# Gate weights loaded in both partition halves, GpSimd's copies placed between its loads, early work ordered by landings: funnel attention followed by a multiplicative FFN

## The chip, the core and the metric

One core of a Trainium2 chip runs the whole program. The metric is the device time of one execution in microseconds, the median of several runs. The core's engines are TensorE (PE, with its weight loads shown apart as PEld), VectorE (DVE), ScalarE (ACT), GpSimd (POOL) and SyncE (SP); each takes its own instructions in order. In this kernel GpSimd issues all loads from memory, and SyncE issues the DMA transposes and nearly all stores.

## The reference

```python
batch, n_heads, seq, head_dim = (8, 8, 1152, 64)
q_pool = q.reshape(B, H, S // 2, 2, D).mean(axis=3)
scores = (1 / sqrt(D)) * np.matmul(q_pool, k.transpose(0, 1, 3, 2))
attn = softmax(scores)                       # along the keys
x = (attn @ v), heads side by side           # 4608 tokens x 512
a = x @ w1                                   # 512 x 1024
b = x @ w2                                   # 512 x 1024
out = ((a * b) @ w3) @ w_out                 # 1024 x 1024, 1024 x 512
```

The inputs are float32, the result is 4608 x 512 float32. The kernel works in float16 with float32 sums; its loads change the type on the way.

## The kernel before

**Attention.** The 64 heads are taken as 32 pairs (a pair P is two heads of one batch, `u` is the head in the pair). A pair has 576 pooled queries and nine blocks of 128 keys, so 9 x 576 = 5184 columns of scores for each head; these columns of all pairs are cut into 324 chunks of 512. A pair is thus 10.125 chunks. For each chunk, `scores` (L274) multiplies keys and queries, one head in each half of the PE's rows, into one of two PSUM buffers `psc`; `expo` (L291) has ACT take the exponential of the 128 x 1024 buffer into the ring `er`. Chunk c+2 cannot be multiplied before the exponential of chunk c has left its buffer. Two bursts per pair, `attend(P, 1)` (36 matmuls) and `attend(P, 0)` (54, L305 and L314), multiply the exponentials with the values `vt`, some 2 and 6 chunks after the pair's last chunk; `normalize` (L329) divides on DVE and issues from SP the DMA transpose of the result `xn` into `xT` (L341), the FFN's input. Where two batches are done, the ninth block of rows goes through `rems` into `xR` (L323) in the same way.

**Preparing a pair.** `load(P)` has GpSimd load k and q of pair P and v of pair P-1 (L116, L108, L123; 288 KB each as float16). For pairs 0 to 8 keys and queries are turned by PE (`prep_stage`, `prep_pe`); `copy_k` puts the keys in order first, on DVE for pairs 1 to 6 and on GpSimd for 7 and 8. From pair 9 on `prep_dma` (L154) does it without PE, all in GpSimd's and SP's queues:

- GpSimd copies the keys into `kc` (L159); SP transposes `kc` into `kT` by DMA (L160);
- GpSimd adds neighbouring queries into `qp` (L143); SP transposes `qp` into `qT` by DMA (L162);
- GpSimd copies the values into `vt` (L152);
- for pairs up to 27, GpSimd copies one element of `kT` into `seen` (L166), which makes its queue wait until the transpose of the keys has landed, and only then issues the loads of pair P+5 and goes on to pair P+1.

**Loads and their semaphores.** GpSimd's loads use eight completion semaphores in turn, so each load waits at its issue until the one eight places before it has landed.

**FFN.** Early on `w3` is turned by PE (`w3_transpose`, L441) and multiplied with `w_out` to `T16` (tile `pT`, L470), once, so that the FFN ends in one product. For each batch `add_unit` (L474) queues 16 gates (`pg`, L506: eight products with `w1` and eight with `w2` into one bank, then a copy and a multiplication into `gT`, L490 and L498) and the row products with `T16` (`pp`, L527). The remainder rows of four batches make a second unit of width 128 behind the first one (batches 3 and 7). A gate's products run in one half of the PE's rows, and the input's heads lie in one half or the other; so `w1sb` and `w2sb` keep each weight twice, once in each partition half. `load_ffn` (L369) loads the first copy; `swap_halves` (L376) makes the second by a product with the permutation matrix `swap` (L384) and a copy on DVE or ACT (L390, L387): 16 of them.

**What sets the order.** The program is written out by hand (`manual_schedule`): a planner in the kernel (L660 to L718) keeps a clock for each PE half and for DVE, emits the next chunk of scores when its exponential is due, and between chunks takes products from the queues `prep` and `ffn` (`step`, L555). What it emits is fixed at build time: each engine runs its instructions in that order, whatever the real landings are. `STAGE`, `PREP`, `early`, `events` and `WEIGHTS` (L637 to L646) say at which point of the pair count or of the planner's clock loads are issued and staged work begins; `ended` (L327) opens a batch's gates 8.0 or 6.5 us (planner's clock) after its last division.

Of the kernel before, what the change touches and what calls it, by code (L numbers as in the profile page):

```python
# [8 lines left out]
FP16 = mybir.dt.float16  # L9
# [14 lines left out]
def kernel(  # L24
# [11 lines left out]
    nc = tc.nc  # L36
# [30 lines left out]
    swap = const.tile([128, 128], FP16)  # L67
# [28 lines left out]
    def take():  # L96
        return spare.pop(0)[1]
# [71 lines left out]
    kcs, kc_done = {}, {}  # L169
# [4 lines left out]

    def prep_stage(P):

        def copy_k(eng=nc.vector):
            eng.tensor_copy(out=new_kc(P).rearrange("p j u d -> p u j d"), in_=kst.pop(P))
        jobs.append((560, lambda: pool_q(P)))
        if P < 7:  # L180
            jobs.append((280, copy_k))
        else:
            copy_k(nc.gpsimd)
            kc_done[P] = max(clock) + 3.0
# [36 lines left out]
    def prep_rest(tb):  # L221
        nc.vector.tensor_copy(out=kcs[0][:, 3:NJ].rearrange("p j u d -> p u j d"),
                              in_=kst[0][:, :, 3:NJ])
        keys(0, tb, range(3, NJ))
        nc.vector.tensor_copy(out=kT[0][:, 3:NJ].rearrange("p j f -> p (j f)"),
                              in_=tb[:, 0:768])
        copy_v(0)
        del kst[0], kcs[0]
# [134 lines left out]
    def load_w(dst, src):  # L363
        nc.gpsimd.dma_start(out=dst, in_=src.rearrange("(c p) f -> p c f", p=128))

    def load_ffn(h):
        cols = slice(512 * h, 512 * h + 512)
        for dst, src in ((w1sb, moe_w1), (w2sb, moe_w2)):
            nc.gpsimd.dma_start(out=dst[:, 0, :, cols],  # L369
                                in_=src.rearrange("(c p) f -> p c f", p=128)[:, :, cols])  # L370
            swaps[h].extend((dst, c, cols) for c in range(NC))

    swaps = ([], [])
    copied = [[1e9], [1e9]]

    def swap_halves():  # L376

        half = 0 if swaps[0] else 1  # L380
        dst, c, cols = swaps[half].pop(0)
# [3 lines left out]
        clock[:] = [max(clock) + 0.22] * 2  # L385
        if c % 3 == 1:
            nc.scalar.copy(out=dst[:, 1, c, cols], in_=t)  # L387
            done = exp_done[-1] = max(exp_done[-1], clock[0] + T_SEM) + 0.6
        else:
            nc.vector.tensor_copy(out=dst[:, 1, c, cols], in_=t)  # L390
            done = vector(512, clock[0])
        give(n, done)
        if not swaps[half]:
            copied[half][0] = done + T_SEM

    def swap_due():
        half = 0 if swaps[0] else 1
        free = 3 if prep[0] or prep[1] else 2
        return bool(swaps[half]) and max(clock) > WEIGHTS[half] and len(spare) >= free and (
            spare[0][0] < min(clock))  # L400

    w3T = {}

# [37 lines left out]
    def w3_transpose(c):  # L441

        w3T[c] = ffp.tile([128, NF, 128], FP16, tag="w3T", bufs=4, name="w3T")
        ready = [1e9]
        left = [2]
        landed = 13.0

        def out(t, at, h):
            nc.vector.tensor_copy(out=w3T[c][:, :, 64 * h:64 * h + 64],
                                  in_=t[:, 0:512].rearrange("p (a f) -> p a f", f=64))  # L450
            done = vector(256, at)
            left[0] -= 1
            if left[0] == 0:
                ready[0] = max(done + T_SEM, landed)
# [9 lines left out]
        def copy(t, at):  # L464
            nc.vector.tensor_copy(out=T16[:, c, :], in_=t)
            del w3T[c]
            return vector(512, at)

        def product(t, s, n, start, stop):
            nc.tensor.matmul(t, w3T[c][s, n, :], wosb[s, n, :], start=start, stop=stop,  # L470
                             skip_group_check=True)
        add(ffn, Block("pT", NF, (0, 1), copy), 0.216, [ready], product)

    def add_unit(n, x, places, ready, final=False):  # L474
# [7 lines left out]
        def gate(ft, h):  # L482
            def mul(t, at):
# [8 lines left out]
                if h not in gT:  # L492
                    gT[h] = ffp.tile([128, NF, 256], FP16, tag="g", bufs=4, name="gT")
# [10 lines left out]
            def emit(t, s, i, start, stop):  # L504
# [5 lines left out]
                [ready, copied[2 * ft // NF]], emit)  # L510
# [24 lines left out]
        for h in range(2):  # L535
            for ft in range(NF):
                gate(ft, h)
# [3 lines left out]
    def add_batch(b, ready):  # L541

        k, o, end = (b // 2) % 2, 256 * (b % 2), b == B - 1
        add_unit(256, lambda s, m: xT[s, m, k, o:o + 256],
                 [(h, 128 * i, [(b, 4 * i + 2 * h), (b, 4 * i + 2 * h + 1)])
                  for h in range(2) for i in range(2)], ready)
        if b % 4 == 3:
            add_unit(128, lambda s, m: xR[s, m // 2, b // 2 - 1:b // 2 + 1, m % 2],
                     [(h, 0, [(b - 3 + h, 8), (b - 1 + h, 8)]) for h in range(2)],
                     ready, final=end)  # L550
# [63 lines left out]
    load_v(0)  # L614
# [3 lines left out]
    load_w(wosb, moe_w_out)  # L618
# [4 lines left out]
    nc.gpsimd.tensor_copy(out=swap[:, 0:64], in_=ident[:, 64:128])  # L623
    nc.gpsimd.tensor_copy(out=swap[:, 64:128], in_=ident[:, 0:64])
# [3 lines left out]
    def last_chunk(P):  # L628
        return -(-(P + 1) * PAIR // CH) - 1

    def copy_v_later(P):
# [8 lines left out]
    events = sorted(  # L640
        [(0.0, 4, load), (0.0, 3, load_w3), (0.4, 5, load), (0.4, 0, load_ffn), (1.2, 6, load),
         (1.2, 1, load_ffn), (2.3, 7, load), (4.0, 8, load), (4.75, 9, load), (5.0, 10, load),
         (5.95, 11, load), (6.95, 12, load), (7.05, 13, load)]
        + list(zip((1.75, 2.6, 3.7, 4.35, 5.1, 5.4, 6.1, 7.0), range(1, NPE),
                   [copy_v_later] * NPE)), key=lambda e: e[0])
    WEIGHTS = (47.0, 57.0)  # L646
    jobs = []
    kq_done[0] = 0.0
    bursts = sorted([(last_chunk(P) + (2 if u == 1 else 6), P, u)
                     for P in range(NP) for u in range(2)])  # L650

    def due(c):


        if bursts and (c + 1) * CH > bursts[0][1] * PAIR + RING:
            return 1e9
        P = ((c + 1) * CH - 1) // PAIR
        return max(exp_done[c - 2] if c > 1 else 0.0, kq_done.get(P, 0.0))
# [3 lines left out]
    while c < NCHUNK or bursts or ffn[0] or ffn[1]:  # L662
        h = 0 if clock[0] <= clock[1] else 1
        if bursts and (c > bursts[0][0] or c == NCHUNK) and spare and spare[0][0] < clock[h] and (
                fresh or c > bursts[0][0] + 1 or c == NCHUNK):
            attend(*bursts.pop(0)[1:])
            fresh = False
            while swap_due():
                swap_halves()
            continue  # L670
        if c >= NCHUNK or due(c) > clock[h]:
# [5 lines left out]
            if not step(h):  # L677
                if swap_due():
                    clock[:] = [max(clock) + 0.1] * 2
                    swap_halves()  # L680
                    clock[:] = [clock[0] + 0.1] * 2
                else:
                    clock[h] += 0.02
# [10 lines left out]
        exp_done.append(max(exp_done[-1] if c else 0.0, max(clock) + T_SEM) + T_EXP)  # L694
        if c == 0:
            prep_rest(rest)
        if jobs:
            n, job = jobs.pop(0)
            job()
            vector(n, 0.0)  # L700
        if staged < NPE and at >= STAGE.get(
                staged, staged - (0.95 if staged < 4 else 1.3)):
            prep_stage(staged)
            staged += 1
        while events and at >= events[0][0]:
            _, n, act = events.pop(0)
            act(n)
        todo = prepped < NP and at >= PREP.get(prepped, prepped - (
            0.65 if prepped < 4 else 0.9 if prepped < NPE else 1.9))
        if todo and prepped >= NPE:  # L710
            prep_dma(prepped)
            prepped += 1
        elif todo and prepped < staged and prepped in kcs:
            prep_pe(prepped)
            prepped += 1
        elif early and c >= early[0][0] and len(w3T) < 4:
            w3_transpose(early.pop(0)[1])
# [38 lines left out]
```

## Time and profile before

| what | value |
|---|---|
| median of 3 runs | 425.18 us (424.91 to 425.28) |
| the profiled execution | 422.81 us, of which the span is 420.7 us |
| PE busy | 402.0 us, 7666 matmuls |
| ACT busy | 330.7 us, 382 instructions; the 324 exponentials are 308.2 us of it |
| DVE, POOL busy | 219.9 us, 191.6 us |
| loads by GpSimd's queue | 33.56 MB, 51.8% of 16 DMA engines' time |
| transposes and stores by SP's queue | 24.22 MB, 36.5% |
| read from memory | 67.11 MB |

Busy times are sums over the span. The PE shows as busy nearly everywhere since its matmuls overlap; how dense it is can be read from the distance of their starts (gate products start 0.11 us apart, one in each half). The last exponential begins at 367.35 us; what follows, up to 416.9 us, is products of the last batches.

### The profile page before, as it was taken

The page shows a single profiled execution, that of the slowest core. Times are in us where ns is not written, and L with a number is a line of the kernel's source. Part 1 is how long each engine was busy: PE and PEld are TensorE (multiplying, and loading weights), DVE is VectorE, ACT ScalarE, POOL GpSimd, SP SyncE. Part 2 cuts the span into 40 slices and gives each one's busy share as a digit, 9 for nine tenths or more (in the row PEclk, how much of TensorE's full clock was granted, in tenths as well). Part 3 has the DMA queues.
Part 4 walks back from the last instruction along what each step waited for, and adds up shares of the span by engine and source line. Part 5 has one row for each costly group of instructions (what it writes and reads, how often), then busy time and mean ns, then how long its engine had stood idle before and what let it go on. Part 6 is the DMA issues. An engine that isn't in the chain of part 4 may idle for free.

```text
span 420.7 us, 17427 instructions
## 1 busy us (share of the span) xinstructions
PE 402.0 (96%) x7666; PEld 320.2 (76%) x7666; DVE 219.9 (52%) x596; ACT 330.7 (79%) x382; POOL 191.6 (46%) x209
## 2 busy tenths in 40 slices
PE   3799999999999999999999997999999999999996
PEld 1366665678778877888788886888878887888894
DVE  3266656876436654664356455466446644542432
ACT  3968888988888888888788896889888888834342
POOL 8243345762564675665645764556688100000000
PEclk9999999999999999999999999999999999999999
DMA  8999999999999999989999999999997422102021
GB/s 120 204 207 201 186 205 200 180 170 142 141 169 185 161 148 164 184 136 121 156 198 130 150 167 186 145 145 173 119 147 160 52 45 92 44 19 101 2 104 51
DMA packets 94219, 59.02 MB, mean 140 GB/s; under 512 B 64832, under 2 KB 84544, under 8 KB 94144
## 3 DMA queue, kind: packets, MB, share of 16 engines
q0 software_dynamic: 26528, 33.56, 51.8%
q1 hardware_dynamic: 67456, 24.22, 36.5%
q8 instruction: 60, 0.98, 1.0%
q10 hardware_dynamic: 160, 0.13, 0.1%
q14 instruction: 15, 0.12, 0.1%
HBM read 67.11 MB, written 9.44 MB: 182 GB/s over the span
## 4 chain that ended last, share of the span: by engine, by line
PE 92%; ACT 3%; DMA 2%; issue 1%; DVE 0%; POOL 0%; ACTq 0%; POOLq 0%
PE pg L506 30%; PE psc L287 19%; PE po L305 18%; PE pp L527 14%; PE pT L470 4%; PE po L314 3%; ACT er L293 3%; PE t L255 1%; DMA xT<-xn 1%; PE sw L384 1%; DMA kst<-in_k_dram 1%; PE w3t L458 0%; PE pp L593 0%; POOL qst L108 0%; PE tb L188 0%
## 5 line engine op out<-in xcount | busy, mean ns | idle before, releaser
L293 ACT ACTIVATE er<-psc 128x1024 f16<-128x1024 f32 x324 | 308.2, 1029 | 49.8 <-PE psc L287 43.7
L287 PE MATMUL psc<-qT,kT 64*128 64x384 f16 (+7 forms) x1152 | 132.3, 291 | 3.9 <-ACT er L293 3.5
L506 PE MATMUL pg<-xT,w2sb 64*128 64x256 f16 x1024 | 129.3, 269 | 0.0
L506 PE MATMUL pg<-xT,w1sb 64*128 64x256 f16 x1024 | 128.4, 269 | 1.0 <-DMA xT<-xn 0.9
L506 PEld LDWEIGHTS <-w1sb 64*128 64x128 f16 x1280 | 102.0, 94 | 9.9 <-issue 1.6
L506 PEld LDWEIGHTS <-w2sb 64*128 64x128 f16 x1280 | 102.0, 94 | 6.0
L527 PE MATMUL pp<-T,gT 64*128 64x512 f16 (+1 forms) x552 | 98.2, 376 | 0.0
L305 PEld LDWEIGHTS <-er 128*128 128x128 f16 x2304 | 74.6, 98 | 18.4 <-issue 15.3
L305 PE MATMUL po<-vt,er 128*128 128x65 f16 x2304 | 82.5, 194 | 2.8 <-issue 2.5
L287 PEld LDWEIGHTS <-kT 64*128 64x128 f16 x1152 | 60.9, 95 | 30.5 <-issue 15.9
L498 DVE TENSOR_TENSOR gT<-pg,asb 128x256 f16<-128x256 f32 (+1 forms) x160 | 66.2, 416 | 24.1 <-ACT asb L487 19.9
L490 DVE COPY asb<-pg 128x256 f32<-128x256 f32 (+1 forms) x119 | 48.1, 404 | 27.4 <-PE pg L506 25.7
L333 DVE RECIPROCAL rz<-po 128x4 f32<-128x4 f32 x64 | 12.1, 189 | 92.8 <-PE po L305 48.2
L143 POOL TENSOR_TENSOR qp<-qst 64x1152 f16<-64x1152 f16 x23 | 54.4, 2367 | 1.0
L527 PEld LDWEIGHTS <-gT 64*128 64x128 f16 (+1 forms) x552 | 43.0, 94 | 11.1
L166 POOL COPY seen<-kT 1x1 f16<-1x1 f16 x19 | 3.4, 181 | 83.6 <-DMA kT<-kc 83.6
L152 POOL COPY vt<-vst 128x1152 f16<-128x1152 f16 x28 | 32.1, 1149 | 6.6 <-issue 5.4
L123 POOL DMA_DIRECT2D vst<-in_v_dram x32 | 23.2, 725 | 19.1 <-DMA kst<-in_k_dram 7.2
L116 POOL DMA_DIRECT2D kst<-in_k_dram x33 | 24.0, 728 | 11.8 <-DMA kst<-in_k_dram 2.7
L487 ACT COPY asb<-pg 128x256 f32<-128x256 f32 (+1 forms) x41 | 13.1, 331 | 19.7 <-PE pg L506 18.6
L336 DVE TENSOR_TENSOR xn<-po,rz 128x256 f16<-128x256 f32 x64 | 27.2, 424 | 2.2
L159 POOL COPY kc<-kst 128x1152 f16<-128x1152 f16 x23 | 26.8, 1164 | 0.8 <-DMA kT<-kc 0.8
(62 smaller groups left out, 254.2 us busy)
## 6 DMA issues: line engine op xcount, KB each, us to landing
qst<-in_q_dram POOLq DMA_DIRECT2D x32, 288.0 KB, 6.9
vst<-in_v_dram POOLq DMA_DIRECT2D x32, 288.0 KB, 8.3
kst<-in_k_dram POOLq DMA_DIRECT2D x31, 288.0 KB, 6.0
out_dram<-osb SPq DMA_DIRECT2D x32, 256.0 KB, 3.4
w3h<-in_moe_w_dram POOLq DMA_DIRECT2D x4, 512.0 KB, 14.5
wosb<-in_moe_w_out_dram POOLq DMA_DIRECT2D x1, 1024.0 KB, 13.8
xT<-xn SPq DMA_TRANSPOSE x64, 4.7
w1sb<-in_moe_w_dram POOLq DMA_DIRECT2D x2, 512.0 KB, 15.6
```

The source lines that it names most:

```text
L116: nc.gpsimd.dma_start(out=kst[P][:, :, js[0]:js[1], :], in_=k[b, h0:h0 + 2].rearrange("u (p j) d -> p u j d", j=NJ)[:, :, js[0]:js[1], :])
L143: (eng or nc.vector).tensor_tensor(out=qps[pp][r].rearrange("p c u d -> p u c d"), in0=src[:, :, :, 0, :], in1=src[:, :, :, 1, :], op=ALU.add)
L152: (eng or nc.vector).tensor_copy(out=vts[P % 4][:, :, :, 0:D], in_=vst.pop(P))
L159: nc.gpsimd.tensor_copy(out=kc.rearrange("p j u d -> p u j d"), in_=kst.pop(P))
L287: nc.tensor.matmul(t[:, u, o:o + ln], kT[P][s, j, :], qv[s, f0:f0 + ln], start=True, stop=True)
L293: nc.scalar.activation(out=er[:, :, r:r + CH], in_=psc.pop(c), func=AF.Exp, bias=0.0, scale=SCALE)
L305: nc.tensor.matmul(po[:, VW * i:VW * i + D + 1], er[:, u, r:r + 128], vts[P % 4][:, u, j, 0:D + 1], start=(j == 0 and i == 0), stop=(j == ...
L336: nc.vector.tensor_tensor(out=xn, in0=acc[:, 0:4, 0:D], in1=rz[:, 0:4].to_broadcast([128, 4, D]), op=ALU.mult)
L490: nc.vector.tensor_copy(out=a, in_=t[:, 0:n])
L498: nc.vector.tensor_mul(out=g, in0=b, in1=a)
L506: nc.tensor.matmul(t[:, n * w:n * w + n], (w1sb, w2sb)[w][s, (m + h) % 2, m // 2, fs], x(s, m), start=start, stop=stop, skip_group_check=True)
L527: nc.tensor.matmul(t, gT[h][s, i, cs], T16[s, i, :], start=start, stop=stop, skip_group_check=True)
```

## The change

The second copy of each gate weight is loaded from memory, the two partition halves by a DMA each, in place of the 16 exchanges; the matrix `swap` goes. `w_out` is loaded in two halves of columns, and the first two products `pT` are made in two halves that wait for them. v of pair 0 is loaded after `w_out`. Loads and GpSimd's copies stand in one list `events`, at fixed places; `copy_k` of pairs 7 and 8 is one of them. Staging of pairs 1 to 8 and the transposes of `w3` are emitted by the planner's clock (`STAGE`, `W3`), looked at before each chunk (`landed`). In the batches with a remainder unit, its gates alternate with those of the first unit, and their tiles use the buffers `w3T` in place of `g`. `prep_dma` and its queueing are the same.

```diff
     def load_ffn(h):
         cols = slice(512 * h, 512 * h + 512)
         for dst, src in ((w1sb, moe_w1), (w2sb, moe_w2)):
+            heads = src.rearrange("(c s p) f -> s p c f", s=2, p=64)[:, :, :, cols]
             nc.gpsimd.dma_start(out=dst[:, 0, :, cols],
                                 in_=src.rearrange("(c p) f -> p c f", p=128)[:, :, cols])
-            swaps[h].extend((dst, c, cols) for c in range(NC))
-    def swap_halves():
-        n = take()
-        t = bank("sw", n)
-        nc.tensor.matmul(t, swap, dst[:, 0, c, cols], start=True, stop=True)
...
+            for s in range(2):
+                nc.gpsimd.dma_start(out=dst[64 * s:64 * s + 64, 1, :, cols], in_=heads[1 - s])
...
             add(ffn, Block("pg", 2 * H, (h,), mul), 0.0025 + n / 2400,
-                [ready, copied[2 * ft // NF]], emit)
+                [ready, [WEIGHTS[2 * ft // NF]]], emit)
...
+        gates = [next(u) for u in units]
         for h in range(2):
             for ft in range(NF):
-                gate(ft, h)
+                for gate in gates:
+                    gate(ft, h)
...
-    load_v(0)
     load_k(1)
     load_q(1)
     load_w3(0)
-    load_w(wosb, moe_w_out)
+    for half in range(2):
+        load_w_out(slice(256 * half, 256 * half + 256))
+    load_v(0)
     load(2)
...
+    def landed(c):
+        nonlocal staged, prepped
+        if vec < max(clock) + 0.3:
+            job()
+        if staged < NPE and max(clock) >= STAGE[staged] and kq_done.get(staged - 1, 1e9) < 1e9:
+            prep_stage(staged)
+            staged += 1
+        if prepped < staged:
+            if not jobs:
+                prep_pe(prepped)
+                prepped += 1
+        elif early and max(clock) >= W3[early[0] // 2] and len(w3T) < 4:
+            w3_transpose(early.pop(0))
...
-    early = [(14, 0), (14, 1), (19, 2), (20, 3), (26, 4), (27, 5), (33, 6), (34, 7)]
-    STAGE = {1: 0.39, 2: 1.4, 3: 2.15, 4: 2.85, 5: 3.85}
-    PREP = {1: 0.55, 2: 1.6, 3: 2.45, 4: 3.2, 5: 4.1}
-    WEIGHTS = (47.0, 57.0)
+    W3 = (5.6, 19.4, 26.4, 32.0)
+    STAGE = {1: 3.2, 2: 15.4, 3: 22.4, 4: 29.4, 5: 36.5, 6: 51.3, 7: 66.3, 8: 70.7}
+    events = [
+        (0.0, load_k, 4), (0.0, load_q, 4), (0.0, load_w3, 3), (0.4, load_v, 3), (0.4, load_k, 5),
+        (0.4, load_q, 5), (0.4, load_ffn, 0), (0.4, load_v, 4), (0.8, load_k, 6),
+        (0.8, load_q, 6), (0.8, load_ffn, 1), (1.15, copy_v_later, 0), (1.75, copy_v_later, 1), (1.8, copy_v_later, 4),
...
+        (5.3, copy_v_later, 5), (5.3, copy_k, 7), (5.3, load_v, 8), (5.4, load_k, 10),
+        (5.4, load_q, 10), (5.4, copy_v_later, 6), (5.4, copy_k, 8), (5.4, load_v, 9),
+        (5.4, load_k, 11), (5.4, load_q, 11), (5.4, copy_v_later, 7), (5.4, load_v, 10),
+        (6.4, load, 12), (6.4, copy_v_later, 8), (6.9, load, 13)]
+    WEIGHTS, WOUT = (47.5, 62.5), (9.2, 11.8)
```

In the built program PE loses the 16 products with `swap` and their weight loads, and makes 64 products `pT` of 256 columns where 32 of 512 were; DVE loses 12 copies of 512 columns and ACT four; GpSimd issues eight loads of 256 KB and one more for `w_out`, and makes two small copies less. SP has the same 168 instructions, in nearly the same order.

More of the change, by code (lines that the diff above doesn't have):

```diff
@@ L368, in load_ffn @@
         for dst, src in ((w1sb, moe_w1), (w2sb, moe_w2)):
+            heads = src.rearrange("(c s p) f -> s p c f", s=2, p=64)[:, :, :, cols]
             nc.gpsimd.dma_start(out=dst[:, 0, :, cols],
                                 in_=src.rearrange("(c p) f -> p c f", p=128)[:, :, cols])
[L371 to L400 removed]
+            for s in range(2):
+                nc.gpsimd.dma_start(out=dst[64 * s:64 * s + 64, 1, :, cols], in_=heads[1 - s])
     w3T = {}
+    second = []
     class Block:
@@ L462, in w3_transpose, with columns, copy, product @@
                 0.0285, [[0.0]], emit)
[L464 to L474, printed above, removed]
+        def columns(cols, landed):
+            m = cols.stop - cols.start
+            def copy(t, at):
+                nc.vector.tensor_copy(out=T16[:, c, cols], in_=t[:, 0:m])
+                if cols.stop == dm:
+                    del w3T[c]
+                return vector(m, at)
+            def product(t, s, n, start, stop):
+                nc.tensor.matmul(t[:, 0:m], w3T[c][s, n, :], wosb[s, n, cols], start=start,
+                                 stop=stop, skip_group_check=True)
+            add(ffn, Block("pT", NF, (0, 1), copy), 0.0025 + m / 2400, [ready, [landed]], product)
+        if c > 1:
+            columns(slice(0, dm), 0.0)
+            return
+        columns(slice(0, 256), WOUT[0])
+        second.append(lambda: columns(slice(256, 512), WOUT[1]))
+        if c == 1:
+            for part in second:
+                part()
+    def unit(n, x, places, ready, final=False):
         gT = {}
@@ L533, in rows @@
                     lambda i: [gdone[h][i]], emit)
-        for h in range(2):
-            for ft in range(NF):
-                gate(ft, h)
+        yield gate
         for h, o, to in places:
```

95 lines of the change are left out of this document (39 added, 56 removed).

## The prediction, made before the changed kernel had run

> **What bounds the kernel now.** I read the chain of waits first (the page's part 4), then ScalarE's timeline, then the chain in order of time at the two places where that timeline breaks step, then SyncE's and GpSimd's timelines there.
>
> ```profile
> PE 92%; ACT 3%; DMA 2%; issue 1%; DVE 0%; POOL 0%; ACTq 0%; POOLq 0%
> ```
>
> The PE carries the chain, but its timing is that of the exponentials. ScalarE's timeline (start, length, engine, line, operation, tiles, count, idle time before and its releaser):
>
> ```profile
> 203.25 2.85 ACT L293 ACTIVATE er<-psc 128x1024 f16<-128x1024 f32 x3 [0.51 <-PE psc L287]
> 207.18 1.02 ACT L293 ACTIVATE er<-psc 128x1024 f16<-128x1024 f32 x1 [1.08 <-PE psc L287]
> 209.12 5.76 ACT L293 ACTIVATE er<-psc 128x1024 f16<-128x1024 f32 x6 [0.91 <-PE psc L287]
> 215.38 3.77 ACT L293 ACTIVATE er<-psc 128x1024 f16<-128x1024 f32 x4 [0.51 <-PE pg L506]
> 219.98 5.76 ACT L293 ACTIVATE er<-psc 128x1024 f16<-128x1024 f32 x6 [0.82 <-PE psc L287]
> ```
>
> From 209.12 to 219.98 is an undisturbed pair: ten chunks in 10.86 us, so 11.0 us for a pair's 10.125; the short idles are the two bursts. The idle of 1.08 before 207.18 is no burst. There the chain in order of time (start, length) says
>
> ```profile
> 200.91 4.88 DMA xT<-xn
> ```
>
> The gates of batch 3 need the transposed result of pair 15. SyncE's and GpSimd's timelines show why it starts so late:
>
> ```profile
> 196.97 2.04 SPq L160 DMA_TRANSPOSE kT<-kc  x1
> 199.30 1.52 SPq L162 DMA_TRANSPOSE qT<-qp  x1
> 200.91 1.21 SPq L341 DMA_TRANSPOSE xT<-xn  x1
> ```
> ```profile
> 193.50 0.18 POOL L166 COPY seen<-kT 1x1 f16<-1x1 f16 x1 [5.03 <-DMA kT<-kc]
> ...
> 195.78 1.16 POOL L159 COPY kc<-kst 128x1152 f16<-128x1152 f16 x1
> 196.90 2.38 POOL L143 TENSOR_TENSOR qp<-qst 64x1152 f16<-64x1152 f16 x1
> ...
> 203.53 0.18 POOL L166 COPY seen<-kT 1x1 f16<-1x1 f16 x1 [3.17 <-DMA kT<-kc]
> ```
>
> In SyncE's order that transpose stands behind keys and queries of pair 18, and these wait for GpSimd. GpSimd runs a loop of its own: `seen` waits for the transposed keys, then three loads (2.1 us), the next keys' copy (1.16), their transpose. Its rounds start at 102.21 (pair 9) and, twelve later, at 237.45: 11.27 us each, no shorter than a pair's 11.0. So it runs free and cannot catch up; all it has is its lead. When it starts:
>
> ```profile
> 12.03 0.72 POOL L116 DMA_DIRECT2D kst<-in_k_dram  x1 [1.67 <-DMA kst<-in_k_dram]
> ...
> 35.38 0.77 POOL L369 DMA_DIRECT2D w1sb<-in_moe_w_dram  x1 [2.15 <-DMA w3h<-in_moe_w_dram]
> ...
> 88.39 0.72 POOL L123 DMA_DIRECT2D vst<-in_v_dram  x1 [2.81 <-DMA kst<-in_k_dram]
> 89.11 1.16 POOL L159 COPY kc<-kst 128x1152 f16<-128x1152 f16 x1
> ...
> 102.21 0.18 POOL L166 COPY seen<-kT 1x1 f16<-1x1 f16 x1 [8.28 <-DMA kT<-kc]
> ```
> ```profile
> 92.27 1.63 SPq L341 DMA_TRANSPOSE xT<-xn  x1
> 94.00 2.86 SPq L160 DMA_TRANSPOSE kT<-kc  x1
> ```
>
> Every load waits for the landing of the one eight before it: up to here the loads are one saturated queue, and pair 9's copy of keys stands behind it. Last, the chain at 258 us:
>
> ```profile
> 258.36 2.53 issue
> ```
>
> There the PE waits for nothing visible, in the middle of the 128-wide gates, its densest stretch of instructions (28 to 40 such products between two chunks, where 256-wide gates have 14 to 20).
>
> **The change, part by part.**
>
> *More loads, and the loop (the path).* The second copies are 2 x 2 loads per half of the columns, 256 KB each: 2,048 KB more, all ahead of pair 9 in the queue. The queue's rate from the rows above: between 12.03 and 35.38 the eleven loads from q of pair 1 to the third part of w3 landed, 4,576 KB in 23.35 us, 196 KB/us; between 35.38 and 88.39, 27 loads (five of 512 KB, 22 of 288), 8,896 KB in 53.0 us, 168 KB/us. So the added loads cost 10.5 to 12.2 us; I take 11.0, nearer the emptier end, since they stand at the border of the two stretches. Against that, the copy of pair 9's keys ended at 90.27 and its transpose waited until 94.00 behind the result of pair 6 (92.27). In the changed order it stands ahead of that result and of the burst before it: 3.7 us regained. The loop starts 11.0 - 3.7 = 7.3 us later. `prep_dma` is unchanged, so nine rounds later pair 18's queries, and the transpose behind them, are 7.3 late too: it lands at 205.79 + 7.3 = 213.1 where the PE waits for it. The PE reaches this wait half a chunk earlier in its work and has as little left behind it; no correction. **+7.3** (bounds: rounds vary from 9.5 to 13.0 us, so nine of them by some 3 us: +4 to +10.5). Queued behind the waiting products: the burst of pair 16 and chunk 178, thus ScalarE.
>
> *The front.* The 16 exchanges with ACT's four copies (0.59 each) and DVE's twelve (0.68) leave chunks 50 to 75. From 61.65 to 107.72 forty chunks took 46.1 us where four pairs take 43.4: 2.6 us to be had at most. The first burst ran 2.16 us against 1.27 for later ones; work now stands ahead of it, 0.9 at most. Losses: transposes of pair 1 now stand behind chunk 3, where the PE must wait for queries that landed at 13.06 and now, v of pair 0 being behind them, some 1.5 us earlier, plus 1.2 us on DVE: about 1.1 us, where the old place cost 0.5. Pair 2's key copies stand on DVE behind copies to `T16` and of v, and 32 transposes of w3 stand ahead of chunk 20 on PE: about 1.4 us. Together some -0.8 (from -3.5 to +1.5). **It counts 0**: what the PE gains before chunk 177 it spends there, waiting for the transpose. If that were on time, the cover would be gone and the front would count.
>
> *Split products `pT`.* 64 of 256 columns for 32 of 512, the same columns; 32 more weight loads (94 ns) run beside products, in a stretch that waits for exponentials. 0. GpSimd's nine more issues (0.72 each) lie in time in which its queue waits for landings. 0.
>
> *Alternating gates.* The 128-wide products no longer follow each other. The wait of 2.53 us should go: **-2.5** (bounds 0 and -2.5; the stretch becomes 1.5 times, not twice, as dense in instructions as 256-wide gates).
>
> *The end.* 372 products of 256 columns stand behind the last scores where 379 did: 7 x 0.11 / 2 = **-0.4**.
>
> Sum against the profiled execution: 422.81 + 7.3 - 2.5 - 0.4 = 427.2 us. The median of the runs shown is 2.4 above that execution, which I carry over: **429.6 us**. Later the loop doesn't bind again: pair 27's keys landed at 306.61, 5.9 us before their chunk; 7.3 late with the PE 4.8 late leaves 3.4.
>
> **The rivals.**
>
> *1. The loop absorbs it (the other side: faster).* If pair 18 is no later than before, the wait at 205 is the old one: 425.18 - 2.5 - 0.4 = 422.3. It decides while the loop's delay at pair 18 is under 2.9 us. For it: rounds as short as 9.5 us occur. Against: the mean of twelve is 11.27, and nothing else in its rows waits for the PE.
>
> *2. The visible wait of 2.5 us stays.* For it: the alternating stretch is still dense. Against: nowhere else is such a wait. 432.1.
>
> *3. Half absorbed.* Shorter rounds give back 3.6 us: 429.6 - 3.6 = 426.0.
>
> *4. Transfers into 64 partitions are slower.* q's loads go into 64 partitions and take 6.9 us from issue to landing, k's 6.0 for as many bytes: with 15% more the added loads take 12.7 us, 1.7 more: 431.3. Against: v's, into 128, take 8.3. The Trainium skill ("DMA: Bandwidth & Descriptors", Rules for kernel authors) speaks against this change: transfers to disjoint partition halves serialize, and one of 128 partitions and at least 1 MiB is best. From its table of bandwidths (138 GB/s at 64 KB, 341 at 1 MB) I estimate that 256 KB loads might run at half the rate; the added loads would then be 22 us and the sum 441. The rows of q so far don't bear that out.
>
> *That it doesn't do what it says* can be left out: the built program has the loads and lacks the exchanges.
>
> **How the numbers follow.** Forecast 0.46, rival 1 0.26, rival 2 0.10, rival 3 0.13, rival 4 0.05. The forecast's own range is 427.0 to 432.0 (the delay 4.7 to 9.7). The 8-in-10 range reaches down into rival 1 and up over rival 2: 422.0 to 432.6; below lies under half of rival 1, above some 0.06. A change under 0.2% (0.85 us) can't be told from none here. Faster: rival 1 and a little of 3, less what of 1 comes out small: 0.28. Same: 0.08. Slower: 0.64.
>
> **What would show it.** Right: the first `seen` near 109.5 us in place of 102.21; an idle of some 7 us on ScalarE before chunk 178, with `xT` as its cause; no wait of 2.5 us near the 128-wide gates; the last exponential near 372 in place of 367.35; the weights' last load landing some 11 us later. Wrong: `seen` starting before 105 (the queue is faster than its rows, or loads wait differently), rounds clearly under 11 us, or a wait at a pair's first scores (keys or queries late) that comes before the one at batch 3. If the front's losses exceed 7 us, the PE reaches chunk 177 later than the transpose, and the reason would be wrong even if the time were right.

## The result and the profile after

The changed kernel takes 431.0 us (median of 17 runs, 425.67 to 436.98) beside 425.18 us for the kernel before in the same session (17 runs, 421.93 to 427.69): a ratio of 1.0137 with a 95% interval of 1.0106 to 1.0168, some 5.8 us slower. Ratios here and below are of the fast runs alone (those within 1.5% of their kernel's fastest), medians are of all runs. The profiled execution of the changed kernel took 425.67 us, the lowest of its 17; of before it took 422.81. So that one profile shows only 2.9 us of the loss, and the experiments below begin with a second one.

The chain of waits of the changed kernel, by engine and by line, then its groups for the exponentials, the gates and `seen` (busy time, mean ns, idle time before and its cause):

```profile
span 423.5 us, 17454 instructions
...
PE 69%; DMA 24%; POOL 3%; issue 1%; DVE 1%; ACT 0%; POOLq 0%; DVEq 0%; SPq 0%; ACTq 0%
...
L290 ACT ACTIVATE er<-psc 128x1024 f16<-128x1024 f32 x324 | 307.9, 1030 | 55.6 <-PE psc L284 53.9
...
L493 PE MATMUL pg<-xT,w1sb 64*128 64x256 f16 x1024 | 124.4, 270 | 3.7 <-DMA xT<-xn 3.4
...
L165 POOL COPY seen<-kT 1x1 f16<-1x1 f16 x19 | 3.4, 179 | 80.2 <-DMA kT<-kc 80.2
```

DMA had 2% of the chain and has 24%: followed back from a wait in the middle, the chain now leaves PE and runs through GpSimd's loads to the start. That is not 24% more time; ScalarE's idle time, which was 49.8 us, is 55.6.

The start of the loop on GpSimd's timeline, and the chain in order of time there (start, length):

```profile
98.43 0.71 POOL L122 DMA_DIRECT2D vst<-in_v_dram  x1 [1.02 <-DMA kst<-in_k_dram]
99.15 1.16 POOL L158 COPY kc<-kst 128x1152 f16<-128x1152 f16 x1
...
111.01 0.18 POOL L165 COPY seen<-kT 1x1 f16<-1x1 f16 x1 [7.05 <-DMA kT<-kc]
```
```profile
99.15 1.16 POOL kc L158
100.39 2.38 POOL qp L142
102.78 10.41 DMA qT<-qp
```

`seen` of pair 9 ends its wait at 111.01 instead of 102.21. The queries of the pair land still later, at 102.78 + 10.41 = 113.19; before they took 5.7 us from an issue at 96.95. The last load of the weights lands at 74.54 instead of 64.16.

ScalarE's timeline around batch 2's gates, the chain there, and SyncE's timeline:

```profile
160.98 2.85 ACT L290 ACTIVATE er<-psc 128x1024 f16<-128x1024 f32 x3 [0.51 <-PE psc L284]
167.18 1.02 ACT L290 ACTIVATE er<-psc 128x1024 f16<-128x1024 f32 x1 [3.35 <-PE psc L284]
```
```profile
163.92 2.32 DMA xT<-xn
```
```profile
158.57 1.27 SPq L159 DMA_TRANSPOSE kT<-kc  x1
160.90 1.21 SPq L161 DMA_TRANSPOSE qT<-qp  x1
162.63 2.47 SPq L338 DMA_TRANSPOSE xT<-xn  x2
```

The input of pair 11's transpose was there at 154.93. In SyncE's order it stands behind the keys and queries of pair 14, which waited for GpSimd; it was issued at 163.92 and landed at 166.24. ScalarE stood idle for 3.35 us. The wait of 2.53 us with the cause "issue" is gone: the longest with that cause in the chain is 0.68 us, at 83.24. Around 258 us the chain reads:

```profile
256.33 0.41 PE po L311 x18
256.74 0.54 PE psc L284 x8
257.28 1.08 PE pp L514 x10
258.36 0.27 PE psc L284 x4
```

Most of what follows is read from one series (the number in front is that of the experiment): the start of an exponential in a profile less its start in the profile of before (us; positive is later). A step between two columns is time lost or won there. Batch 2's gates lie between 136 and 140, batch 3's between 176 and 184, the old 2.5 us wait between 224 and 228, pair 9's first scores between 88 and 92.

```
chunk                       44    68    92   136   140   180   184   224   228   323
   after, first profile    +1.1  +1.3  +2.4  +2.1  +5.7  +5.1  +5.0  +4.8  +2.0  +2.9
 1 after, second profile   +0.3  -0.4  +2.9  +2.8  +7.7  +7.2 +10.9 +11.3  +8.5  +8.7
 2 no second copies        +3.3   0.0  +0.9  +0.7  +5.2  +3.9  +3.8  +4.1  +1.3  +1.7
 3 no turns                 0.0  -1.5  +1.7  +3.3  +8.2  +7.0  +7.0  +6.7  +6.5  +6.5
 7 keys behind xT          +2.6  +2.0  +6.9  +7.3  +7.6  +7.3  +8.3  +8.7  +5.9  +8.0
 8 six loads later         +1.7  -1.3  +5.5  +5.8 +10.1  +9.1 +10.0 +11.7  +8.9  +9.1
 5 four output tiles       +1.4  -0.4  +2.4  +3.3  +9.3  +8.5  +8.4 +11.2  +8.4  +8.6
 4 before + turns          +0.3  +0.1  +0.1  +0.3  +0.3  -1.0  -1.1  +1.3  -1.5  +4.5
 6 before + weights twice   0.0  +8.3  +9.2  +8.8 +12.5 +11.4 +11.4 +13.4 +10.7 +14.3
10 before + keys behind xT +0.5  +0.3  +0.4  +0.2  +0.2  -1.1  -1.1  -1.1  -2.2  -2.2
 9 keys behind xT, split   +3.2  +2.1  +7.1  +6.6  +6.6  +5.7  +7.1  +8.0  +5.2  +5.5
11 before + all three      +0.8  +0.6  +0.8  +0.5  +0.5  -0.8  -0.9  +0.3  -2.5  -2.1
12 no second, keys behind  +1.4  -2.0  -1.3  -1.8  -1.8  -3.2  -2.8  +0.4  -2.4  -2.1
```

### The profile page after: what moved, and what is told of

It reads as the page before. It is cut to its first block, busy times and chain, and to the rows that moved or that the text cites. A ratio compares the mean times of both kernels' runs of the same rounds, so it can differ in the third digit from the quotient of the medians.

```text
span 423.5 us, 17454 instructions
## 1 busy us (share of the span) xinstructions
PE 399.2 (94%) x7682; PEld 316.9 (75%) x7682; DVE 210.3 (50%) x589; ACT 328.1 (77%) x377; POOL 196.9 (46%) x216
## 4 chain that ended last, share of the span: by engine, by line
PE 69%; DMA 24%; POOL 3%; issue 1%; DVE 1%; ACT 0%; POOLq 0%; DVEq 0%; SPq 0%; ACTq 0%
PE pg L493 26%; PE pp L514 14%; PE psc L284 13%; PE po L302 13%; DMA kst<-in_k_dram 10%; DMA w1sb<-in_moe_w_dram 7%; DMA vst<-in_v_dram 3%; DMA qT<-qp 2%; PE po L311 2%; DMA xT<-xn 2%; POOL qp L142 1%; POOL vst L122 0%; POOL qst L107 0%; POOL wosb L361 0%; PE pp L585 0%
## 5 line engine op out<-in xcount | busy, mean ns | idle before, releaser
L290 ACT ACTIVATE er<-psc 128x1024 f16<-128x1024 f32 x324 | 307.9, 1030 | 55.6 <-PE psc L284 53.9
L284 PE MATMUL psc<-qT,kT 64*128 64x192 f16 (+7 forms) x1152 | 130.1, 289 | 4.7 <-ACT er L290 3.2
L493 PE MATMUL pg<-xT,w1sb 64*128 64x256 f16 x1024 | 124.4, 270 | 3.7 <-DMA xT<-xn 3.4
L493 PE MATMUL pg<-xT,w2sb 64*128 64x256 f16 x1024 | 126.1, 270 | 0.0
L493 PEld LDWEIGHTS <-w1sb 64*128 64x128 f16 x1280 | 92.7, 94 | 11.5 <-issue 4.1
L493 PEld LDWEIGHTS <-w2sb 64*128 64x128 f16 x1280 | 92.0, 94 | 5.6
L514 PE MATMUL pp<-T,gT 64*128 64x512 f16 (+1 forms) x552 | 94.1, 376 | 0.0
L476 DVE COPY asb<-pg 128x256 f32<-128x256 f32 x120 | 48.4, 404 | 28.0 <-PE pg L493 26.8
L514 PEld LDWEIGHTS <-gT 64*128 64x128 f16 (+1 forms) x552 | 38.6, 94 | 17.4 <-issue 1.2
```

The source lines that it names most:

```text
L284: nc.tensor.matmul(t[:, u, o:o + ln], kT[P][s, j, :], qv[s, f0:f0 + ln], start=True, stop=True)
L290: nc.scalar.activation(out=er[:, :, r:r + CH], in_=psc.pop(c), func=AF.Exp, bias=0.0, scale=SCALE)
L476: nc.vector.tensor_copy(out=a, in_=t[:, 0:n])
L493: nc.tensor.matmul(t[:, n * w:n * w + n], (w1sb, w2sb)[w][s, (m + h) % 2, m // 2, fs], x(s, m), start=start, stop=stop, skip_group_check=True)
L514: nc.tensor.matmul(t, gT[h][s, i, cs], T16[s, i, :], start=start, stop=stop, skip_group_check=True)
```

## The experiments

All ratios are to the kernel before in the same session, with 95% intervals. A median is that of all runs of the kernel, with their range. The median of the kernel before was 425.2 to 425.8 in the sessions of experiments 1 to 11 and 423.25 in that of experiment 12, so kernels of different sessions are better compared by their ratios.

**1. The changed kernel again.**

> The changed kernel once more, unchanged. Its first profiled execution took 425.67 us and its median is 431.0, so most of what the change costs is not in that profile. Theory (GpSimd's loop starts late and then runs with little slack, 1.3 to 2.2 us ahead of the first scores of pairs 9 to 13): a slower execution shows longer waits of PE on landings of xT, kT or qT between chunks 88 and 180, 2 to 6 us more of them than the 3.4 us at batch 2's gates of the first profile. Rival (a general slowing, of every matmul or every exponential): the waits are the same and the pace between them, 10.86 us for ten chunks, is longer. Median again 429 to 433 us.

Measured: 430.92 us (429.62 to 439.73, 6 runs), 1.0119 [1.0058, 1.018]; the profiled execution took 431.43. The second row of the table says where: +3.8 at pair 9's first scores (first profile +1.2), +4.9 at batch 2's gates (+3.6), and a new +3.7 between 180 and 184. From chunk 92 on the two rows run parallel to within 0.6 us between these places, so the rival (a slower pace everywhere) falls. The new one is on the chain as

```profile
210.27 7.54 DMA out_dram<-osb
```

A store of output rows, itself issued behind transposes in SyncE's queue, lands late; VectorE waits for its tile and PE for VectorE. The theory holds for two of the three places; this third is not a landing of `xT`, `kT` or `qT`.

**2. No second copies.**

```diff
-            for s in range(2):
-                nc.gpsimd.dma_start(out=dst[64 * s:64 * s + 64, 1, :, cols], in_=heads[1 - s])
...
-  (w1sb, w2sb)[w][s, (m + h) % 2, m // 2, fs]
+  (w1sb, w2sb)[w][s, 0, m // 2, fs]
```

> The changed kernel without its eight loads of the second copies (2,048 KB fewer); every gate reads the first copy, so half of its products take the wrong half of the weights. The order of TensorE's instructions is that of the changed kernel. Theory (the loads delay GpSimd's queue): the first wait for pair 9's transposed keys is over near 101 us instead of 111, the wait for xT at batch 2's gates is gone, and the time falls by 5 to 9 us, to 422 to 426, that is to before or under it by the 2.5 us of the alternating gates. Rival (the new order of PE and of the front costs the time): 429 to 432 us, as the changed kernel.

Measured: 426.56 us (422.37 to 432.36, 12 runs), 0.998 [0.9946, 1.0013]. The time falls by 4.4 us (by the ratios, 1.0119 to 0.998, by the whole loss) and the wait at pair 9's first scores is gone (+0.1 between 88 and 92). But `seen` of pair 9 comes at 107.17, not 101, and the step at batch 2's gates stays at 4.5 us. So the loads are more than half of the loss. Whether they alone make the wait for `xT` this profile can't say: its `seen` is still 5.0 us later than in the kernel before. Experiment 12's kernel is this one up to pair 9, and there `seen` came at 101.10; the same loads ahead of it landed up to 6.5 us apart in the two executions.

**3 and 4. The turns, taken out of the changed kernel and put alone into the one before.**

```diff
-        gates = [next(u) for u in units]
-        for h in range(2):
-            for ft in range(NF):
-                for gate in gates:
-                    gate(ft, h)
+        for u in units:
+            gate = next(u)
+            for h in range(2):
+                for ft in range(NF):
+                    gate(ft, h)
```

> The changed kernel with the gates of the remainders behind those of the batch again, in place of taking turns. Theory: PE's wait with the cause issue, 2.5 us in the dense gates of 128 columns near 258 us, comes back, and the time is 2 to 3 us above the changed kernel's, 433 to 434 us. Rival 1 (the wait has gone because the instructions before it have shifted, not because of the turns): no such wait, the same 431 us. Rival 2 (the turns themselves cost, through the shared tiles): 428 to 430 us.

> The kernel before with one part of the change alone: the gates of the remainders taking turns with those of the batch. Loads and exchanges as before. Theory: the 2.5 us wait with the cause issue at 258 us goes, and the time is 1.5 to 3 us under before, 422 to 423.5 us. Rival (the wait moves to another dense stretch, or another wait takes its place at the next landing): within 1 us of before, 424.5 to 426 us.

Measured: without turns 434.37 us (429.22 to 440.84, 6 runs), 1.0144 [1.0085, 1.0202]; before with turns 429.35 us (425.71 to 432.17, 12 runs), 1.0104 [1.0063, 1.0145]. Without the turns the chain again has

```profile
264.35 2.28 issue
```

and the step of -2.8 at 224 to 228 is gone (-0.2). By the ratios the turns are worth 1.1 us here (1.0144 against 1.0119), with intervals that overlap. In the kernel before, the turns won the same 2.8 us there and lost more elsewhere: its time rose by 3.8 us where 1.5 to 3 less were expected. PE's waits and VectorE's (us in total, times, longest) name the place:

```profile
PE pg L507 <- DVE osb L521: 3.4, 1, 3.4
```
```profile
DVE osb L521 <- DMA out_dram<-osb: 8.1, 3, 4.8
```

Another 2.4 us were lost between 184 and 224, where waits with the cause "issue" of 1.28 and 0.88 us now stand at 225.76 and 238.24. The term of 2.5 us is thus right at its place, in all ten profiles with turns; what it is worth in the end depends on the stores and on such new waits, of 0.5 to 1.3 us between 210 and 260 us in five of the ten. What they are is told at the end.

**5. Four output tiles in place of three** (`tag="osb", bufs=4` in the changed kernel).

> The changed kernel with four tiles for output rows on their way to memory in place of three. In its second profile 3.7 us were lost between chunks 180 and 184 where the chain runs through a store of output rows that took 7.5 us, and VectorE waited for its tile. Theory (late stores are a good part of the run-to-run loss): the median falls by 1 to 3 us to 428 to 430, and the spread of the runs (425.7 to 439.7) gets narrower. Rival (they are rare): 430 to 432, same spread.

Measured: 430.08 us (427.2 to 433.49, 6 runs), 1.011 [1.0057, 1.0164]. Within 1 us of the changed kernel; inconclusive as to its size, and small at most.

**6. Weights loaded twice, alone in the kernel before.**

```diff
+            heads = src.rearrange("(c s p) f -> s p c f", s=2, p=64)[:, :, :, cols]
+            for s in range(2):
+                nc.gpsimd.dma_start(out=dst[64 * s:64 * s + 64, 1, :, cols], in_=heads[1 - s])
-            swaps[h].extend((dst, c, cols) for c in range(NC))
...
-            while swap_due():
-                swap_halves()
...
-    copied = [[1e9], [1e9]]
+    copied = [[47.5], [62.5]]
```

> The kernel before with one part of the change alone: the weights loaded twice and no exchanges; the front, the places of GpSimd's copies and the order of the gates as before. Theory (2,048 KB more in GpSimd's saturated queue): pair 9's keys come 7 to 11 us later than 102.2, batch 2's or batch 3's gates wait for xT, and the time is 3 to 7 us over before, 428 to 432. Rival (GpSimd's queue is delayed by the fixed places of its copies, not by the loads): pair 9's keys near 103 to 105 and 424 to 427 us.

Measured: 435.72 us (432.38 to 437.49, 6 runs), 1.0232 [1.0179, 1.0286]: more than the whole change, and more than expected. `seen` of pair 9 came at 112.82, 10.6 us late, as the theory has it. Most of the loss is another wait, though:

```profile
PE po L304 <- POOL vt L151: 8.5, 1, 8.5
```
```profile
72.93 0.72 POOL L122 DMA_DIRECT2D vst<-in_v_dram  x1 [1.84 <-DMA w2sb<-in_moe_w_dram]
73.64 1.16 POOL L151 COPY vt<-vst 128x1152 f16<-128x1152 f16 x1
```

The copy of pair 4's values stands in GpSimd's queue behind loads that wait for landings, and the burst waits for it. In the changed kernel this copy has a fixed place further forward (61.0 us), and the longest such wait is 0.6 us: the second part of the change takes this wait away.

**7. Keys and queries behind `xT` in SyncE's queue** (from pair 10 on; GpSimd's order is untouched).

```diff
-        if NPE <= prepped < NP and at >= prepped - 1.9:
+        if NPE <= prepped < NP and at >= prepped - (1.9 if prepped == NPE else 1.45):
```

> The changed kernel with the keys' and queries' transposes from pair 10 on put behind, not ahead of, the transposes xT of the pair three before in SyncE's queue (0.45 pairs later in the order). GpSimd's order is the same. Theory: xT of pair 11 is issued when its input is there (155 instead of 164 us) and batch 2's gates no longer wait: the step of 3.5 to 4.9 us between chunks 136 and 140 goes, and the time is 3 to 5 us under the changed kernel's 431. Rival 1 (keys then come too late): a wait at the first scores of pairs 12 to 14, and no gain. Rival 2 (the gates wait for something else than the order of SyncE's queue): the step stays.

Measured: 428.53 us (423.97 to 430.75, 12 runs), 1.0067 [1.0022, 1.0113]; 2.5 us under the changed kernel. The step between 136 and 140 falls to 0.3 us, on SyncE's timeline because

```profile
156.12 5.41 SPq L338 DMA_TRANSPOSE xT<-xn  x2
162.07 2.60 SPq L159 DMA_TRANSPOSE kT<-kc  x1
```

the results go first. The wait at pair 9's first scores is still there (+4.1 in this profile); pairs 12 to 14 don't wait, and of the later ones only one does, 1.02 us for its queries at 298.14.

**8. Six loads moved behind pair 9's keys and queries.**

```diff
         nc.sync.dma_start_transpose(
             out=qT[P], in_=qps[pp][o:o + 64].rearrange("p c u d -> p (c u d)"))
+        if P == 9:
+            load(12)
+            copy_v(8, nc.gpsimd)
+            load(13)
...
-        (6.4, load, 12), (6.4, copy_v_later, 8), (6.9, load, 13)]
```

> The changed kernel with the loads of pairs 12 and 13 (six, 1,728 KB) moved behind pair 9's copy of keys and sum of queries in GpSimd's queue. Theory: pair 9's transposed keys come when the loads ahead of them have landed (in five profiles their wait was over 0.2 to 0.9 us after the landing of the last load before it, at 101.8 to 111.9 us), so it is over near 101 us instead of 111, the 2 to 4 us lost at pair 9's first scores (chunks 88 to 92) come back, and the wait for xT at batch 2's gates gets shorter: 2 to 5 us under the changed kernel's 431. Rival (transposes share the DMA engines with whatever loads are under way, also those issued later): the wait still ends at 109 to 111 and the time stays within 1 us of the changed kernel's.

Measured: 437.94 us (431.83 to 447.2, 6 runs), 1.0237 [1.0168, 1.0306]: worse. The keys were issued at 90.84 instead of 100.33 but `seen` came at 106.90, after 16 us, and of the queries the chain says

```profile
93.30 21.79 DMA qT<-qp
```

They landed at 115.09; the last of the loads issued meanwhile landed at 115.20. So a transpose does not only wait for the loads issued before it: the rival is right in kind, these transposes share the engines with whatever is under way. It had neither number, though: `seen` came 2 us before the 109 to 111 it gave, and the time rose by more than its 1 us. By the Trainium skill ("DMA: Bandwidth & Descriptors", Queues, rings and completion order) each DMA engine takes packets in turn from the queues that it has work for; the 21.79 us agree with that, and a queue of its own didn't shield the transpose.

**9. Keys behind `xT`, and the loads of pair 13 behind pair 9's `seen`.**

```diff
             nc.gpsimd.tensor_copy(out=seen[:, 0:1], in_=kT[P][0:1, 0, 0:1])
+            if P == 9:
+                load(13)
             load(P + 5)
...
-        (6.4, load, 12), (6.4, copy_v_later, 8), (6.9, load, 13)]
+        (6.4, load, 12), (6.4, copy_v_later, 8)]
```

> The changed kernel with the later place of keys and queries in SyncE's queue, and with the three loads of pair 13 (864 KB) behind pair 9's seen instead of ahead of its copy of keys. Theory (pair 9's transposed keys and queries land when the loads issued before them, and those still issued after them, have landed): seen of pair 9 comes 3 to 5 us earlier, near 106 to 108 us, its first scores wait 0 to 1 us instead of 2 to 4, and the time is 1.5 to 4 us under the 428.5 with the later place alone. Rival (the loads come in the way of pair 10's or 11's transposes instead): seen of pair 9 is earlier, but the wait is at pair 10's or 11's first scores, and the time is 428 to 430.

Measured: 426.35 us (423.55 to 432.38, 12 runs), 1.0049 [0.9998, 1.0099]. The wait at pair 9's first scores is gone (+0.2 between 88 and 92; its keys were 6.4 us early). `seen` was not earlier, 111.46: this execution's front was 3 us late, and the keys' copy began at 101.10. The queries landed at 111.96, 4.9 us before those of experiment 7. But the loss has moved: 3.6 us stand between chunks 84 and 88, at a wait of 2.23 us with the cause "issue" at 109.23, and at chunk 92 both profiles are some 7 us behind. The 2.2 us between the medians are 0.8 by the ratios, with intervals that overlap: the theory is not shown.

**10 and 11. The kernel before with keys behind `xT`** (the same line), **and that with turns and four output tiles as well.**

> The kernel before with one thing changed: from pair 10 on the transposes of keys and queries stand behind, not ahead of, xT of the pair three before in SyncE's queue. Theory (xT of pair 15 stands behind pair 18's keys and queries, and batch 3's gates wait 1.1 us for it): that wait goes, 0.5 to 1.5 us under before, 424 to 425.3. Rival (keys then come later at every round, and the lead of GpSimd's loop is used up): waits at first scores, 425.6 to 428.

> The kernel before with three things: the gates in turns, the later place of keys and queries in SyncE's queue, and four tiles for output rows. With the turns alone, VectorE waited 8.1 us for stores of output rows, PE 4.4 us for VectorE, and the 2.8 us gained at chunk 228 were lost again at chunks 196 to 244. Theory (the three tiles for output rows, and stores behind transposes in SyncE's queue, are what the turns run into): these waits go, and the time is 2 to 5 us under before, 421 to 424. Rival (the turns cost in another way): 426 to 430 as with the turns alone.

Measured: 420.23 us (418.89 to 423.12, 12 runs), 0.9909 [0.9876, 0.9943], and 421.26 us (418.95 to 424.73, 12 runs), 0.9956 [0.9917, 0.9995]. Both beat both kernels. The one line of order is worth 5.0 us by the medians and 3.9 by the ratio (2.4 to 5.3), where 0.5 to 1.5 were expected. ScalarE's timeline of experiment 10 no longer has the idle of 1.08 us at batch 3's gates:

```profile
197.07 5.83 ACT L293 ACTIVATE er<-psc 128x1024 f16<-128x1024 f32 x6
203.41 3.77 ACT L293 ACTIVATE er<-psc 128x1024 f16<-128x1024 f32 x4 [0.51 <-PE psc L287]
208.01 5.76 ACT L293 ACTIVATE er<-psc 128x1024 f16<-128x1024 f32 x6 [0.82 <-PE psc L287]
```

The table has -1.3 there and -1.1 at 228 (the wait with the cause "issue" is 1.48 us instead of 2.53), and 2.2 at the end. What the ratio has beyond these 2.2 us no profile shows, and it stays open. In experiment 11 the turns' loss at the stores is gone for the most part (6.0 between 228 and 323 became 0.4), which bears the reading of experiment 4 out; three edits were made there at once, so it is not said which did it. Turns on top of the order gain nothing that these runs can tell (0.9956 against 0.9909).

**12. No second copies, and keys behind `xT`.**

> The changed kernel without the loads of the second copies (every gate reads the first copy, so half of its products take the wrong half of the weights), and with keys and queries behind xT in SyncE's queue from pair 10 on. It closes the sum: if the extra loads (through pair 9's keys and queries) and the order of SyncE's queue (through xT at batch 2's and 3's gates) are together what the change runs into, neither wait is left, the step of 4.5 us at chunks 136 to 140 that the kernel without the second copies still had is gone, and the time is 419 to 422.5 us, 4 to 7 under that kernel's 426.6 and near the 420.2 of the kernel before with the same order. Rival (the new front, or PE's new order, has a price of its own): 423.5 to 427.

Measured: 423.58 us (419.03 to 429.56, 12 runs), 0.9994 [0.9956, 1.0031]. The median is 3.0 us under that of experiment 2, but the median of the kernel before, taken beside it, was 2.3 us lower too; by the ratios (0.998 there) the order gains nothing here. In the profile both waits are gone and the sum closes: no step at pair 9 nor at batch 2, and 2.1 us under before at the end, as in experiment 10 (2.2). The time of the runs doesn't close: the median lies at the lower end of the rival's range, 3.3 us over experiment 10 (3.6 by the ratios). From 184 to 224 even this profile loses 3.2 us, among it waits with the cause "issue" of 1.0 us at 211.75 and 223.71, where experiment 10 loses nothing; whether that is what the other runs lose wasn't tried.

## Why the prediction was right, and where it was not

The direction and the time were right (429.6 forecast, 431.0 measured, in the forecast's own range), and so was the source of the loss, the added loads. The place was not: the forecast put the whole loss at batch 3's gates, an idle of 7 us before chunk 178, and there PE waited 0.25 us. That the sum came out near is in part luck. By its steps:

- **More loads, and the loop: right in kind, near in size.** The weights landed 10.4 us later against 11.0, and `seen` of pair 9 came at 111.01 against 109.5 (8.8 us late, not 7.3). Loaded twice alone, the weights made it 10.6 us late. Taken out of the changed kernel, they gave back 3.8 us of `seen` in experiment 2's profile and 9.9 in experiment 12's. One part was worth less than forecast: the 3.7 us regained in SyncE's order were there at the issue (the keys' transpose was issued 0.02 us after their copy). But the transpose took 10.63 us instead of 8.16: it landed only behind the last load ahead of it, and that one landed 9.1 us later than before.
- **"Nine rounds later pair 18's queries, and the transpose behind them, are 7.3 late too": this step failed.** The rounds from pair 9 to 18 took 10.8 us, not 11.3, and `seen` of pair 18 was 4.7 us late; so the loop gave back 4.1 us on the way, which is what rival 3 describes (3.6 there). More to the point, the loss did not wait for batch 3. The forecast said that PE reaches this kind of wait "half a chunk earlier"; with the exchanges gone, PE starts on batch 2's gates while exponential 134 runs instead of 138 (on batch 3's at 174 instead of 175). Four chunks are 4.3 us, and so batch 2's gates, which had not waited, took the wait for `xT`: 3.6 us in one profile, 4.9 in the other. In before the result had landed at 161.00 and the gates began at 163.82, 2.8 us to spare; in after it landed 5.2 us later and the gates began 2.0 us earlier. So the later loop and the earlier place both have their part, and no run parts them (in experiment 2 too the loop was 5 us late at pair 9). Experiment 7 shows that SyncE's order is what makes the transpose late.
- **A wait that the forecast named as a sign against it came.** Pair 9's first scores wait for its queries, 1.2 us in the first profile and 3.8 in the second. The forecast had followed the keys only, which in before landed 8.7 us ahead of these scores. The queries' transpose stands behind the keys' and lands, like theirs, behind the loads under way: at 113.19, 10.5 us later than before, where the scores would have started near 112.3. Experiments 2 and 12, without the added loads, have no such wait.
- **Alternating gates, -2.5: right at its place.** -2.8 in all ten profiles with turns. Without them a wait with the cause "issue" stands near this place in all four: 2.5 us before, 2.3 in experiment 3, 1.5 in 10, and in 6 two, of 1.8 and 1.9 us. That the same edit loses time at the stores in the kernel before, and that smaller waits of the kind come up elsewhere, was not foreseen.
- **The front, 0: not shown to be 0.** At chunk 44 the seven profiles with the new front and the second copies stand 0.0 to 3.2 us behind before, at chunk 68 from -1.5 to +2.1. It varies by more than the forecast's term, and its mean is a loss of 1.5 us at 44 and of 0.3 at 68. The reason for the 0 fell too: with next to no wait left at chunk 177, there was nothing to spend a gain on. (The 43.4 us that the forecast sets against its forty chunks are forty chunks at 1.086 us; four pairs, 40.5 chunks, are 44.0.)
- **The median over the profiled execution, +2.4: mis-sized.** It was 431.0 - 425.67 = 5.3. The forecast's sum of 427.2 for the profiled execution was 1.5 too high, and this term 2.9 too low, so the two errors nearly met: this is the luck. Experiment 1's profile, of an execution of 431.43 us, shows what such a time can consist of, the same waits, longer, and a late store.
- **The rivals.** The loop took back about half of its delay by pair 18, as rival 3 has it, but the time didn't fall with it, since PE had waited before that. The 2.5 us wait didn't stay. Slower loads into 64 partitions are a small part at most: the eight second copies landed one after the other at a mean of 1.52 us for 256 KB, the four first copies at 2.66 us for 512 KB. That makes 12.2 us for the 2,048 KB instead of the 11.0 of the forecast, 168 KB/us for the halves beside 193 for whole loads (over all eight profiles with the second copies, 173 beside 190). The rule of the Trainium skill that the forecast weighed ("DMA: Bandwidth & Descriptors", Rules for kernel authors), that transfers to the two halves serialize, agrees with landings one after the other. The 22 us that the forecast estimated beside it are not borne out.

What stays open: the 3.3 us (3.6 by the ratios) by which the changed kernel without the second copies and with the better order still stands over the kernel before with that order. Its profile doesn't have them.

## What to carry to other kernels

When a queue runs transfers in order, look for the one that the bound engine will ask for first, and what it stands behind: here one line that put results ahead of keys gained the kernel before 3.9 us. Work taken off an engine brings its next consumer forward, so a removed cost can turn a transfer with time to spare into the one that is waited for. And a profile is one execution: a second one of the same kernel had the same two waits, longer by 2.5 and 1.3 us, and a third of 3.7 us that the first did not have.

## What the runs showed of the hardware

- The transposes of pair 9 are issued while loads issued before them are still under way, and landed only behind these. In all 13 profiles but experiment 8's, `seen` came after the last load ahead of it had landed: 0.2 to 0.9 us in ten of them (before 101.27 and 102.21, after 110.35 and 111.01), 2.3 to 2.7 in three. So the same transposes took 8.2 us (keys) and 5.7 (queries) in before, 10.6 and 10.4 in after, and 16.0 and 21.8 in experiment 8, where six more loads were issued behind them.
- PE's waits with the cause "issue" go with the arrival of its instructions. Over the 14 profiles PE has 25 such waits of more than 0.5 us, 15 of them while batch 3's gates run. The page of before, and that of after, shows a queue for instructions (packets, MB, share of 16 engines):

```profile
q8 instruction: 60, 0.98, 1.0%
```

These are 60 packets of 16,384 bytes. Every one of the 25 waits ends 1.3 to 1.8 us after one of them has landed; only 9% of all moments in before are at such a distance. And if PE's products and weight loads are counted in order, all 25 stand at the same place of the count by 256 (remainder 193 to 195); the 15,332 of before are some 256 to a packet. So the 2.53 us at 258.36 in before, the 2.23 us of experiment 9 (its packet took 2.5 us to land) and the waits of experiments 4 and 12 are most likely waits for PE's next block of instructions. Of 60 packets in a profile none to four are waited for. This is read from the traces; no run changed it alone.
